# Key and value gradients of one-query attention: chunk transposes as plain matmuls into 32-bit half tiles, with other PSUM banks

## The chip, the cores and the metric

The kernel runs on one core of a Trainium2 chip. The time is that of the device for one execution, in microseconds (us). Five engines of the core work side by side, each through its own list of instructions in order: TensorE (PE, matrix products; its weight loads are listed apart as PEld), VectorE (DVE), ScalarE (ACT), GpSimd (POOL) and SyncE (SP), which here only issues transfers. Sixteen DMA engines move data between the chip's main memory (HBM) and the core's SBUF; every large transfer is cut over all sixteen. Matrix products land in PSUM, eight banks of 2 KB in each of 128 partitions.

## What is computed

Attention with a single query, and its gradients, for 64 heads (2 x 32), 8192 keys and values of 128 numbers, in bf16:

```python
B, H, Sq, Sk, D = 2, 32, 1, 8192, 128
scores = jnp.einsum("bhqd,bhkd->bhqk", q, k) * scale     # scale = D ** -0.5
p = softmax(scores, axis=-1)
out = jnp.einsum("bhqk,bhkd->bhqd", p, v)
out, vjp = jax.vjp(forward, q, k, v)
return out, *vjp(grad_out)                               # out, dq, dk, dv
```

Written out for one head, with g for grad_out: P = softmax(scale K q), grad P = V g, delta = sum(P grad P), dS = P (grad P - delta). The outputs are out = P V, dq = scale K^T dS, and two outer products as large as the inputs: dv = P g^T and dk = scale dS q^T. K and V are read once (2 MB each for a head) and dk and dv written once (2 MB each): 537 MB for all heads.

## The kernel before

A head's K and V lie in SBUF as tiles `kt` and `vt`, 128 partitions of 64 keys (NT = 64) of 128 numbers. Both pools have five buffers (UNITS). The two outer products are written in place: dv over `vt`, dk over `kt`, and these tiles are stored.

The order of the work is written out by hand (`tc.manual_schedule`, L299): no planner moves anything, each engine executes its instructions in the order of the source, and waits between engines are put in from the tiles that are read and written. The main loop (L302) runs over 65 iterations; in iteration h the scores and grad P of head h (`y`) are made and head h - 1 (`x`, index `p`) is finished. An iteration has eight steps j, one for each chunk of 16 key blocks (CH = 16): steps 0 to 3 work through K, steps 4 to 7 through V.

- `transposes` (L110): TensorE transposes 16 blocks of 128 x 128 into a bf16 PSUM tile `tp` (2 banks, two buffers); ScalarE copies the tile to SBUF as `ev` (L118).
- `products` (L122): one step later, 16 matmuls with a transposed block as weights and the one column q (or g) write 16 columns of `sdpw`. This tile is one bank for a head: scores, grad P, the transposed maxima, the broadcast maximum, the sums and the combined outputs all lie in it; it has two buffers.
- `row_max`, `all_max`, `exps` (steps 4, 5, 6): maximum over the scores, turned and broadcast by TensorE, then Exp on ScalarE with the row sums. `to_weights` casts P into `wz`, a tile that is zero but for 4 of 32 columns, so that eight heads (OG = 8) accumulate in different rows of one bank.
- `deltas`, `sums`, `weights` (steps 0, 1 of the next iteration): delta, 1/l, dS and the factors of the outer products on VectorE.
- `weighted_rows` (L229): 32 matmuls of a head, 512 columns wide, in four column groups of the array, sum P V and dS K into the banks `acc0` and `acc1`. Every eighth head `acc_to_sbuf` and `combine` (8 f32 matmuls) bring out the outputs of eight heads.
- `outer` (L263): eight VectorE products of 128 x 2048 a head, 1.2 us each, one in steps 1, 2, 4, 5, 6 and 7 and two in step 3.
- SP's queue: `store` of dv (step 3), `store` of dk (step 7), then the two loads of head h + 3 (`load`, L108), which need the buffers of head h - 2 and so wait until its stores have landed. The last head is stored in halves.
- `spread_rows` (L136), every fourth head: q and g are broadcast to all partitions through a buffer of `tp`.

PSUM holds two banks `acc`, two `sdpw` and four `tp`.

Of the kernel before, what the change touches and what calls it, by code (L numbers as in the profile page):

```python
# [10 lines left out]
AX = mybir.AxisListType  # L11
BF16 = mybir.dt.bfloat16
F32 = mybir.dt.float32

CH = 16
QG = 4
OG = 8
UNITS = 5
# [3 lines left out]
def kernel(  # L22
# [11 lines left out]
    nc = tc.nc  # L34
# [6 lines left out]
    assert NT * P == Sk and NT == 4 * CH and BH <= P and BH % QG == 0  # L41
    assert BH % OG == 0 and OG * 4 == 32
    NS = 2 * NT // CH
# [9 lines left out]

    pick = const.tile([P, 4, OG], F32)
    idv = ident_f[:].rearrange("p (g k j) -> p g j k", g=4, k=OG)
    nc.vector.tensor_copy(out=pick[:], in_=idv[:, 0])
    for g in range(1, 4):
# [7 lines left out]
    kvp = ctx.enter_context(tc.tile_pool(name="kv", bufs=UNITS))  # L65
    evp = ctx.enter_context(tc.tile_pool(name="ev", bufs=3))
    work = ctx.enter_context(tc.tile_pool(name="work", bufs=2))
    rowp = ctx.enter_context(tc.tile_pool(name="rows", bufs=2))
    ps_acc = ctx.enter_context(tc.tile_pool(name="ps_acc", bufs=1, space=bass.MemoryType.PSUM))
    ps_sdp = ctx.enter_context(tc.tile_pool(name="ps_sdp", bufs=2, space=bass.MemoryType.PSUM))  # L70
    ps_tp = ctx.enter_context(tc.tile_pool(name="ps_tp", bufs=2, space=bass.MemoryType.PSUM))
# [5 lines left out]

    MT0 = 2 * NT
    MB0 = MT0 + P
    LS0 = MB0 + 1  # L80
    CB0 = LS0 + 2
    SDPW = CB0 + 2 * OG

    acc = [ps_acc.tile([P, 4 * D], F32, name=f"acc{i}", tag=f"acc{i}") for i in range(2)]
    qT_all = const.tile([P, BH], BF16)
# [5 lines left out]
    wz = [  # L91
        [const.tile([P, NT // 4, 4 * OG], BF16, name=f"wz{w}{k}") for k in range(OG)]
        for w in range(2)
    ]
    colsT = [const.tile([P, BH], BF16, name=f"colsT{i}") for i in range(2)]
    class Head:
# [12 lines left out]

    def transposes(h, j):  # L110

        x = heads[h]
        w, c = divmod(j, NS // 2)
        tp = ps_tp.tile([P, CH, P], BF16, name="tp", tag="tp")
        for i in range(CH):
            nc.tensor.transpose(tp[:, i, :], x.kv[w][:, c * CH + i, :], ident_bf[:])  # L116
        ev = evp.tile([P, CH, P], BF16, name="ev", tag="ev")
        nc.scalar.copy(out=ev[:], in_=tp[:])  # L118
        x.ev = getattr(x, "ev", {})
        x.ev[j] = ev  # L120

    def products(h, j):  # L122
        x = heads[h]
        w, c = divmod(j, NS // 2)
        if j == 0:
            x.sdpw = ps_sdp.tile([P, SDPW], F32, name="sdpw", tag="sdpw")
            x.sdp = x.sdpw[:, 0 : 2 * NT].rearrange("p (a n) -> p a n", a=2)
        ev = x.ev.pop(j)
        col = (qT_all, doT_all)[w][:, h : h + 1]
        for i in range(CH):  # L130
            n = c * CH + i
            nc.tensor.matmul(  # L132
                x.sdp[:, w, n : n + 1], lhsT=ev[:, i, :], rhs=col, start=True, stop=True
            )
# [18 lines left out]
    def row_max(x):  # L153
        x.mp = work.tile([P, 1], F32, name="mp", tag="mp")
        nc.vector.reduce_max(out=x.mp[:], in_=x.sdp[:, 0, :], axis=AX.X)  # L155

    def all_max(x):
        mT = x.sdpw[0:1, MT0 : MT0 + P]
        nc.tensor.transpose(mT, x.mp[:], ident_f[:])
        x.gm = work.tile([1, 1], F32, name="gm", tag="gm")  # L160
        nc.vector.reduce_max(out=x.gm[:], in_=mT, axis=AX.X)  # L161

    def exps(x):
        mb = x.sdpw[:, MB0 : MB0 + 1]
        nc.tensor.matmul(mb, lhsT=ones_f[0:1, :], rhs=x.gm[:], start=True, stop=True)  # L165
        negm = work.tile([P, 1], F32, name="negm", tag="negm")
        nc.vector.tensor_scalar(out=negm[:], in0=mb, scalar1=-scale, scalar2=None, op0=ALU.mult)  # L167
        x.E = work.tile([P, NT], F32, name="E_f", tag="E_f")
        x.ld = work.tile([P, 2], F32, name="ld", tag="ld")
        nc.scalar.activation(  # L170
            out=x.E[:],
            in_=x.sdp[:, 0, :],
            func=ACT.Exp,
            bias=negm[:],
            scale=scale,
            accum_out=x.ld[:, 0:1],
        )

    def to_weights(h, w, src):
        k = h % OG  # L180
        nc.vector.tensor_copy(  # L181
            out=wz[w][k][:, :, 4 * k : 4 * k + 4],
            in_=src[:].rearrange("p (m j) -> p m j", j=4),
        )

    def deltas(x):
        junk = work.tile([P, NT], BF16, name="junk", tag="junk")
        nc.vector.tensor_tensor_reduce(  # L188
            out=junk[:],
            in0=x.E[:],  # L190
            in1=x.sdp[:, 1, :],
            scale=1.0,
            scalar=0.0,
            op0=ALU.mult,
            op1=ALU.add,
            accum_out=x.ld[:, 1:2],
        )

    def sums(x):
        x.lsum = x.sdpw[:, LS0 : LS0 + 2]  # L200
        nc.tensor.matmul(x.lsum, lhsT=ones_f[:], rhs=x.ld[:], start=True, stop=True)  # L201

    def weights(h):
# [10 lines left out]
        nc.vector.scalar_tensor_tensor(  # L214
            out=dSu[:], in0=x.sdp[:, 1, :], scalar=negdelta[:], in1=x.E[:],
            op0=ALU.add, op1=ALU.mult,
# [12 lines left out]
    def weighted_rows(h, w, chunks):  # L229


        rows, k = heads[h].kv[1 - w], h % OG
        for c in chunks:
            for g in range(4):
                n = c * CH + 4 * g
                nc.tensor.matmul(  # L236
                    acc[w][32 * g : 32 * g + 32, :],
                    lhsT=wz[w][k][:, n // 4, :],
                    rhs=rows[:, n : n + 4, :].rearrange("p n d -> p (n d)"),
                    start=(k == 0 and c == 0),  # L240
                    stop=(k == OG - 1 and c == NT // CH - 1),
                    tile_position=(0, 32 * g),
                )

    def acc_to_sbuf(x, w):
        sb = work.tile([P, 4 * D], F32, name="accsb", tag=f"accsb{w}", bufs=1)
        nc.vector.tensor_copy(out=sb[:], in_=acc[w][:])  # L247
        x.accsb = getattr(x, "accsb", {})
        x.accsb[w] = sb

    def combine(h, w):

        x = heads[h]
        c = x.sdpw[:, CB0 + w * OG : CB0 + (w + 1) * OG]
        for j in range(4):
            nc.tensor.matmul(  # L256
                c, lhsT=x.accsb[w][:, j * D : (j + 1) * D], rhs=pick[:, j, :],
                start=(j == 0), stop=(j == 3),
            )
        own = slice(h - OG + 1, h + 1)  # L260
        nc.vector.tensor_mul(out=colsT[w][:, own], in0=c, in1=rl_all[:, w, own])  # L261

# [36 lines left out]
    with tc.manual_schedule():  # L299
        for h in range(min(UNITS, BH)):  # L300
            load(h)
        for h in range(BH + 1):  # L302
# [4 lines left out]
            for j in range(NS):  # L307
                if y:
                    transposes(h, j)
                if x and j == 1:  # L310
                    sums(x)
                if y and j == 5:
                    all_max(y)
                if y and j == 6:
                    exps(y)
                if x and j < 4:
                    weighted_rows(p, j // 2, (2 * (j % 2), 2 * (j % 2) + 1))
                if x and j == 0:
                    products(p, NS - 1)
                    deltas(x)  # L320
                if y and j:
                    products(h, j - 1)
                if y and j == 4:
# [3 lines left out]
                if x:  # L327
                    if j == 1:
                        weights(p)
                        outer_and_store(p, 0, 0)  # L330
                    elif j == 2:
                        outer_and_store(p, 0, 1)
                    elif j == 3:
                        outer_and_store(p, 0, 2)
                        outer_and_store(p, 0, 3)
                    elif j > 3:
                        outer_and_store(p, 1, j - 4)
                    if full and j in (4, 5):
                        acc_to_sbuf(x, j - 4)
                    if full and j in (6, 7):  # L340
                        combine(p, j - 6)
                if j == 7:
# [4 lines left out]
        for w, dst in enumerate((o_rows, dq_rows)):  # L347
            tps = ps_tp.tile([BH, P], BF16, name="tps", tag="tp")
            nc.tensor.transpose(tps[:], colsT[w][:], ident_bf[:])
            rows = const.tile([BH, D], BF16, name=f"rows{w}")  # L350
            nc.scalar.copy(out=rows[:], in_=tps[:])
            nc.scalar.dma_start(out=dst, in_=rows[:])
# [30 lines left out]
```

## Time and profile before

| | |
|---|---|
| Time, median of 3 runs | 1311.24 us (1307.66 to 1312.27) |
| The profiled execution | 1311.96 us, span 1310.2 us |
| TensorE busy / weight loads | 1088.4 us (83%) / 893.3 us (68%) |
| ScalarE, VectorE, GpSimd busy | 984.5 us (75%), 746.9 us (57%), 8.5 us (1%) |
| Mean granted TensorE clock | 0.828 |
| Moved between HBM and SBUF | 268.5 MB read, 268.5 MB written, 410 GB/s over the span |

The profile is one execution, recorded by the hardware. Its page gives the busy time of each engine, the busy time in 40 equal slices with the granted clock and the DMA rate, the chain of work that ended last, and groups of instructions by source line: line, engine, operation, output <- input, shape, count, then busy time and mean duration in ns, then the idle time in front and what ended it. The trace behind it can be asked for stages (busy time of PE, PEld, DVE, ACT and POOL, then clock, DMA share, GB/s), for waits (who waited for whom: us in total, times, longest) and for transfers (count, KB each, median us from issue to landing). A DMA share of 1.00 says that all sixteen engines had a packet under way, not at which rate. Times are in us from the start of the span.

### The profile page before, as it was taken

The numbers are of one execution on the slowest core, as the hardware profiler recorded it, in microseconds if no ns is written. First come the engines' busy times: TensorE is split into PE (matmuls) and PEld (weight loads), VectorE is DVE, ScalarE is ACT, GpSimd is POOL, SyncE is SP. The second block draws the span as 40 slices with busy tenths as digits, with TensorE's granted clock in tenths as the row PEclk, the third lists the DMA queues.
The fourth block names the chain that finished last, engine by engine and source line by source line (L and its number), as shares of the span: only waits on it lengthen the run. The fifth ranks groups of instructions, "written<-read, shape, count | busy, mean of one in ns | idle before, by whom it ended". The sixth has DMA issues, their size and how long they took to land.

```text
span 1310.2 us, 41065 instructions
## 1 busy us (share of the span) xinstructions
PE 1088.4 (83%) x18948; PEld 893.3 (68%) x18948; DVE 746.9 (57%) x1383; ACT 984.5 (75%) x659; POOL 8.5 (1%) x24
## 2 busy tenths in 40 slices
PE   5888888888888888888888888888888888888783
PEld 4766776766776766766777676776777766666672
DVE  2655646655655655556556556465565656465564
ACT  5777868878778776778868788688777878687771
POOL 2000000000000000000000000000000000000000
PEclk9887879888888887878878789788888889798885
DMA  9999999999999999999999999999999999999995
GB/s 396 405 379 427 406 428 402 425 427 428 427 428 428 428 429 427 403 429 426 426 410 415 429 426 427 418 417 427 425 412 419 423 414 408 407 408 403 406 371 231
DMA packets 37644, 539.57 MB, mean 412 GB/s; under 512 B 4448, under 2 KB 4448, under 8 KB 4448
## 3 DMA queue, kind: packets, MB, share of 16 engines
q1 hardware_dynamic: 37152, 536.89, 97.9%
q8 instruction: 148, 2.42, 0.7%
q14 instruction: 24, 0.20, 0.0%
q10 hardware_dynamic: 320, 0.07, 0.0%
HBM read 268.47 MB, written 268.47 MB: 410 GB/s over the span
## 4 chain that ended last, share of the span: by engine, by line
PE 57%; ACT 23%; DMA 12%; DVE 4%; issue 2%; ACTq 0%; SPq 0%
PE tp L116 31%; ACT ev L118 22%; PE sdpw L132 13%; PE acc L236 10%; DMA out_dram<-kt 7%; DMA kt<-in_k_dram 4%; DVE kt L268 3%; PE sdpw L256 2%; ACT E_f L170 1%; PE sdpw L201 1%; DMA nat<-in_grad_out_dram 1%; PE pb L141 1%; DVE accsb L247 0%; DVE gm L161 0%; DVE vt L268 0%
## 5 line engine op out<-in xcount | busy, mean ns | idle before, releaser
L118 ACT COPY ev<-tp 128x2048 bf16<-128x2048 bf16 x512 | 947.8, 1866 | 290.0 <-PE tp L116 273.8
L132 PEld LDWEIGHTS <-ev 128*128 128x128 bf16 x8192 | 260.9, 99 | 328.8 <-issue 244.3
L116 PE MATMUL tp<-ident_bf,kt 128*128 128x128 bf16 x4096 | 340.9, 250 | 12.9 <-DMA kt<-in_k_dram 7.1
L116 PE MATMUL tp<-ident_bf,vt 128*128 128x128 bf16 x4096 | 311.9, 237 | 0.8 <-issue 0.8
L268 DVE TENSOR_TENSOR kt<-qd,dS 128x2048 bf16<-128x2048 bf16 x256 | 310.5, 1213 | 0.2 <-DVE mp L155 0.2
L116 PEld LDWEIGHTS <-kt 128*128 128x128 bf16 x4096 | 296.0, 114 | 19.6 <-issue 11.0
L268 DVE TENSOR_TENSOR vt<-qd,P 128x2048 bf16<-128x2048 bf16 x256 | 295.8, 1216 | 0.0
L132 PE MATMUL sdpw<-doT_all,ev 128*128 128x1 bf16 x4096 | 145.2, 165 | 172.6 <-ACT E_f L170 128.5
L116 PEld LDWEIGHTS <-vt 128*128 128x128 bf16 x4096 | 268.6, 107 | 1.0 <-issue 1.0
L188 DVE CUSTOM_DVE_ANT_0 junk<-E_f,sdpw 128x64 bf16<-128x64 f32 x64 | 14.1, 221 | 293.1 <-PE sdpw L132 293.1
L132 PE MATMUL sdpw<-qT_all,ev 128*128 128x1 bf16 x4096 | 141.6, 164 | 6.3 <-ACT ev L118 2.4
L236 PE MATMUL acc<-vt,wz 128*32 128x512 bf16 x1024 | 100.0, 476 | 0.0
L236 PE MATMUL acc<-kt,wz 128*32 128x512 bf16 x1024 | 81.3, 397 | 0.1
L236 PEld LDWEIGHTS <-wz 128*32 128x32 bf16 x2048 | 32.1, 98 | 27.8 <-issue 12.3
L206 DVE RECIPROCAL rl_all<-sdpw 128x1 f32<-128x1 f32 x64 | 10.8, 168 | 70.0 <-PE sdpw L201 70.0
L155 DVE TENSOR_REDUCE mp<-sdpw 128x1 f32<-128x64 f32 x64 | 14.4, 224 | 57.6 <-PE sdpw L132 57.6
L167 DVE TENSOR_SCALAR negm<-sdpw 128x1 f32<-128x1 f32 x64 | 10.1, 158 | 43.0 <-PE sdpw L165 42.2
L181 DVE CAST wz<-E_f 128x64 bf16<-128x64 f32 x64 | 12.4, 194 | 38.9 <-ACT E_f L170 38.9
L256 PE MATMUL sdpw<-pick,accsb 128*128 128x8 f32 x128 | 29.5, 359 | 5.8 <-DVE accsb L247 4.8
L256 PEld LDWEIGHTS sdpw<-pick,accsb 128*128 128x128 f32 x128 | 28.3, 325 | 6.8 <-DVE accsb L247 5.7
L261 DVE TENSOR_TENSOR colsT<-sdpw,rl_all 128x8 bf16<-128x8 f32 x16 | 2.7, 166 | 38.6 <-PE sdpw L256 38.6
L165 PE MATMUL sdpw<-gm,ones_f 1*128 1x1 f32 x128 | 24.2, 256 | 0.0
(39 smaller groups left out, 304.4 us busy)
## 6 DMA issues: line engine op xcount, KB each, us to landing
kt<-in_k_dram SPq DMA_DIRECT2D x64, 2048.0 KB, 24.8
vt<-in_v_dram SPq DMA_DIRECT2D x64, 2048.0 KB, 29.3
out_dram<-vt SPq DMA_DIRECT2D x63, 2048.0 KB, 25.7
out_dram<-kt SPq DMA_DIRECT2D x63, 2048.0 KB, 23.0
out_dram<-vt SPq DMA_DIRECT2D x2, 1024.0 KB, 12.7
out_dram<-kt SPq DMA_DIRECT2D x2, 1024.0 KB, 12.0
out_dram<-rows ACTq DMA_DIRECT2D x2, 16.0 KB, 5.7
nat<-in_q_dram ACTq DMA_DIRECT2D x1, 16.0 KB, 8.0
```

The lines of the kernel that those rows point to most:

```text
L116: nc.tensor.transpose(tp[:, i, :], x.kv[w][:, c * CH + i, :], ident_bf[:])
L118: nc.scalar.copy(out=ev[:], in_=tp[:])
L132: nc.tensor.matmul(x.sdp[:, w, n : n + 1], lhsT=ev[:, i, :], rhs=col, start=True, stop=True)
L141: nc.tensor.matmul(pb[:, i].rearrange("p a d -> p (a d)"), lhsT=ident_bf[0:BH, h : h + 1].to_broadcast([BH, P]), rhs=nat[:].rearrange("p a ...
L155: nc.vector.reduce_max(out=x.mp[:], in_=x.sdp[:, 0, :], axis=AX.X)
L165: nc.tensor.matmul(mb, lhsT=ones_f[0:1, :], rhs=x.gm[:], start=True, stop=True)
L170: nc.scalar.activation(out=x.E[:], in_=x.sdp[:, 0, :], func=ACT.Exp, bias=negm[:], scale=scale, accum_out=x.ld[:, 0:1],)
L188: nc.vector.tensor_tensor_reduce(out=junk[:], in0=x.E[:], in1=x.sdp[:, 1, :], scale=1.0, scalar=0.0, op0=ALU.mult, op1=ALU.add, accum_out= ...
L201: nc.tensor.matmul(x.lsum, lhsT=ones_f[:], rhs=x.ld[:], start=True, stop=True)
L236: nc.tensor.matmul(acc[w][32 * g : 32 * g + 32, :], lhsT=wz[w][k][:, n // 4, :], rhs=rows[:, n : n + 4, :].rearrange("p n d -> p (n d)"), ...
L256: nc.tensor.matmul(c, lhsT=x.accsb[w][:, j * D : (j + 1) * D], rhs=pick[:, j, :], start=(j == 0), stop=(j == 3),)
L268: nc.vector.tensor_tensor(out=x.kv[1 - w][:, n : n + CH, :].rearrange("p n (d t) -> p n d t", t=2), in0=row.unsqueeze(1).to_broadcast([P, ...
```

## The change

- Each transpose is a plain matmul with the identity as the moving operand; `tp` is f32 and holds eight blocks (a half chunk, HC = 8) in the same 2 banks. `ev` is a half chunk in bf16, with five buffers for three.
- Of a head's 16 copies of half chunks ScalarE makes 14 and VectorE two: the second halves of steps 0 and 7.
- An iteration's step is split in halves u = 0, 1: transposes, products and weighted rows alternate by half chunk.
- Four heads (OG = 4) share one bank `acc` for both sums: P takes the first 16 of 32 columns of `wz`, dS the last 16. Both outputs of four heads are combined in one bank `c`.
- The scores lie in a bank `sm`, grad P and the sums in a bank `dp`, one buffer each.
- The outer products move: step 1 has one, steps 2 and 3 two, steps 4, 5 and 6 one, step 7 none. Stores are issued behind the same products as before, so in steps 3 and 6.

```diff
-    def transposes(h, j):
+    def transposes(h, j, u):
...
-        tp = ps_tp.tile([P, CH, P], BF16, name="tp", tag="tp")
-        for i in range(CH):
-            nc.tensor.transpose(tp[:, i, :], x.kv[w][:, c * CH + i, :], ident_bf[:])
-        ev = evp.tile([P, CH, P], BF16, name="ev", tag="ev")
-        nc.scalar.copy(out=ev[:], in_=tp[:])
+        tp = ps_tp.tile([P, HC, P], F32, name="tp", tag="tp")
+        for i in range(HC):
+            n = c * CH + u * HC + i
+            nc.tensor.matmul(
+                tp[:, i, :], lhsT=x.kv[w][:, n, :], rhs=ident_bf[:], start=True, stop=True
+            )
+        ev = evp.tile([P, HC, P], BF16, name="ev", tag="ev")
+        if u and j in (0, 7):
+            nc.vector.tensor_copy(out=ev[:], in_=tp[:])
+        else:
+            nc.scalar.copy(out=ev[:], in_=tp[:])
...
-        if j == 0:
-            x.sdpw = ps_sdp.tile([P, SDPW], F32, name="sdpw", tag="sdpw")
-            x.sdp = x.sdpw[:, 0 : 2 * NT].rearrange("p (a n) -> p a n", a=2)
+        if c == 0 and u == 0:
+            if w:
+                x.dp = ps_one.tile([P, NT + 2], F32, name="dp", tag="dp")
+            else:
+                x.sm = ps_one.tile([P, NT + P + 1], F32, name="sm", tag="sm")
...
-            out=wz[w][k][:, :, 4 * k : 4 * k + 4],
+            out=wz[w][k][:, :, 16 * w + 4 * k : 16 * w + 4 * k + 4],
...
-                    acc[w][32 * g : 32 * g + 32, :],
+                    acc[32 * g : 32 * g + 32, :],
...
-                    start=(k == 0 and c == 0),
-                    stop=(k == OG - 1 and c == NT // CH - 1),
+                    start=(w == 0 and k == 0 and c == 0),
+                    stop=(w == 1 and k == OG - 1 and c == NT // CH - 1),
...
             for j in range(NS):
-                if y:
-                    transposes(h, j)
...
+                for u in range(2):
+                    if y:
+                        transposes(h, j, u)
+                    if u == 0:
+                        if x and j == 1:
+                            sums(x)
+                        if y and j == 5:
+                            all_max(y)
+                        if y and j == 6:
+                            exps(y)
+                    if y and j:
+                        products(h, j - 1, u)
+                    elif x and j == 0:
+                        products(p, NS - 1, u)
+                    if x and j < 4:
+                        weighted_rows(p, j // 2, (2 * (j % 2) + u,))
+                if x and j == 0:
+                    deltas(x)
...
                 if x:
-                    if j == 1:
-                        weights(p)
-                        outer_and_store(p, 0, 0)
-                    elif j == 2:
-                        outer_and_store(p, 0, 1)
-                    elif j == 3:
-                        outer_and_store(p, 0, 2)
-                        outer_and_store(p, 0, 3)
-                    elif j > 3:
-                        outer_and_store(p, 1, j - 4)
-                    if full and j in (4, 5):
-                        acc_to_sbuf(x, j - 4)
-                    if full and j in (6, 7):
-                        combine(p, j - 6)
+                    for i in ((), (0,), (1, 2), (3, 4), (5,), (6,), (7,), ())[j]:
+                        outer_and_store(p, i // 4, i % 4)
+                    if full and j == 4:
+                        acc_to_sbuf(x)
+                    if full and j == 6:
+                        combine(p)
```

The remaining lines carry the new names (`x.sm` and `x.dp` for `x.sdp`, one `colsT`, `pick` and `c` with both outputs) through.

## The prediction

> **What bounds the kernel now.** I read the page's totals first, then the busy times by stage, the waits, the transfers by stage, and two single heads. All durations come from the one profiled execution: span 1310.2 us, 1311.96 us as timed, so 1.8 us lie around the span; it stands 0.7 us above the median of 1311.24. A measurement of this kernel can tell about 0.5% (6.6 us) from no change.
>
> The stages, whose last three columns are the granted TensorE clock, the share of the DMA engines and GB/s:
>
> ```profile
> 0.00:60.00 60.00, 41.80 (x679) 34.66 (x680) 24.30 (x43) 37.51 (x25) 8.55 (x24) 0.86 0.98 407
> 60.00:100.00 40.00, 34.56 (x648) 28.20 (x646) 25.07 (x45) 32.82 (x23) 0.00 (x0) 0.87 0.93 375
> 240.00:520.00 280.00, 239.64 (x4179) 197.17 (x4177) 162.45 (x304) 216.49 (x145) 0.00 (x0) 0.83 1.01 428
> 960.00:1240.00 280.00, 235.00 (x4137) 192.77 (x4135) 161.86 (x302) 215.32 (x144) 0.00 (x0) 0.84 1.00 412
> 1240.00:1310.00 70.00, 44.33 (x672) 33.99 (x669) 34.75 (x63) 32.64 (x23) 0.00 (x0) 0.67 0.75 308
> ```
>
> The reader sees that the DMA engines have no idle time from 100 to 1240 us. A head moves 8.39 MB (two loads and two stores of 2.10 MB), so 428 GB/s is 19.6 us for a head. The totals of the waits and, below them, SP's waits in 960 to 1240:
>
> ```profile
> PE sdpw L132 <- ACT E_f L170: 128.5, 64, 2.1
> PE sdpw L132 <- DVE gm L161: 43.4, 64, 1.5
> PE tp L116 <- DMA kt<-in_k_dram: 7.1, 4, 2.4
> ```
>
> ```profile
> SPq L108 <- DMA out_dram<-kt: 196.1, 14, 18.9
> SPq L276 <- DVE kt L268: 53.4, 16, 9.2
> ```
>
> TensorE almost never waits for a load (7.1 us), so compute looks like the bound; yet late in the run the loads themselves stand in SP's queue for 14 us a head, until an old store has landed and freed their buffer. The landing times say why. Issues of 100 to 240, 240 to 520 and 960 to 1240 us, one line of each (last number: us to landing):
>
> ```profile
> out_dram<-kt SPq DMA_DIRECT2D x7, 2048.0 KB, 11.0
> ```
>
> ```profile
> out_dram<-kt SPq DMA_DIRECT2D x14, 2048.0 KB, 20.0
> ```
>
> ```profile
> out_dram<-kt SPq DMA_DIRECT2D x14, 2048.0 KB, 36.1
> ```
>
> The trace holds the 16 completion marks of each transfer, one from each DMA engine. The last mark comes 2.7 us after the first at 65 us, 2.9 at 236, 14.7 at 530, and 17 to 19 from 944 to the end: one engine falls behind steadily. From 236 to 540 us its marks are 5.067 us apart (20.27 us a head) and the foremost engine's 4.86 (19.45). From 78 us its marks follow each other with no step over 6.6 us up to 1309.2, 1 us before the end. So the slowest DMA engine sets the time. Compute matters only where it leaves that engine dry (two steps of 6.2 and 7.8 us behind 64.5), and a second way: when the backlog reaches 18 us, loads wait for it, the other fifteen engines run dry together each head, start together, and 16 KB packets that take 0.611 us then take 0.8 to 1.5 us in bursts. From 944 to 1284 us the slowest engine itself needs 5.159 us a transfer (66 of them in 340.5 us), 20.64 a head.
>
> Two heads show compute, one undisturbed, one in a stretch where the clock fell to 0.5:
>
> ```profile
> 598.80:616.90 18.10, 15.44 (x293) 13.05 (x293) 11.28 (x22) 15.05 (x11) 0.00 (x0) 0.91 1.01 430
> 656.00:682.00 26.00, 23.31 (x327) 19.18 (x324) 12.48 (x25) 15.83 (x12) 0.00 (x0) 0.67 1.01 430
> ```
>
> Store issues at 239.8 and 932.7 us lie 35 heads apart: 19.8 us a head for compute, mixed from such heads.
>
> **The change part by part.** Rows used:
>
> ```profile
> L118 ACT COPY ev<-tp 128x2048 bf16<-128x2048 bf16 x512 | 947.8, 1866 | 290.0 <-PE tp L116 273.8 <-ACT ev L118 1.4
> L149 ACT CAST qd<-pb 128x1024 bf16<-128x1024 f32 x16 | 16.2, 1016 | 8.1 <-PE pb L141 8.1
> L247 DVE COPY accsb<-acc 128x512 f32<-128x512 f32 x16 | 10.8, 678 | 0.0
> L155 DVE TENSOR_REDUCE mp<-sdpw 128x1 f32<-128x64 f32 x64 | 14.4, 224 | 57.6 <-PE sdpw L132 57.6
> ```
>
> *ScalarE.* Eight copies a head of 1.866 us (14.9) become 14 of half size. The L149 row is exactly such a copy, 1.016 us: 14.2 us. With Exp and its sum (0.52) and a quarter of the L149 copy (0.25) ScalarE needs 15.0 us a head, 0.7 less.
>
> *VectorE.* Two copies of 128x1024 are added. From the PSUM rows, (678 - 224)/(512 - 64) is 1.01 ns an element, so 1.2 us each (bounds: 1.016 as ScalarE, 1.36 as twice 678): 2.4 us a head on 11.7 (746.9/64), 14.1 in all. They are hidden while VectorE stays under ScalarE's 15.0. Queued behind each are delta and the weights (at j = 0) and the cast of P (at j = 7); who waits is TensorE at `sums`, and at the next half tile, since the copy holds one of two PSUM buffers. I take 1.2 us a head for that.
>
> *TensorE.* The 128 transposes become as many matmuls with the same operands and columns. Sixteen transposes take 0.92 us at full clock (57.5 ns each). From above: the L141 matmul writes 32-bit output from 256 columns, four in 1.03 us at half clock, so 65 ns for 128 columns at full clock, +1.0 us a head. From below: 16 products with one column take 0.48 us, 30 ns each, -3.5 us. The row with the same columns is nearest, so I take no change. In the trace the clock falls to 0.5 in 64 stretches that sum to 452 us although TensorE is busy 83% of the span. [...]
>
> *Own banks.* The products of grad P no longer write the bank that Exp and the maximum read: 2.0 and 0.7 us a head of waits go. What is late next is ScalarE's chain of half copies, 15.0 us. So a head of compute lies between 15.0 and the present 18.1 us undisturbed; with VectorE's 1.2 us and the wait at `sums` I take 17. With the clock as uneven as now (+1.7, from 19.8 against 18.1) it would be 18.7. Both are under 19.45, so the transfers hide either one.
>
> *Sums of four heads.* The combine in f32 runs 16 times with both outputs in one, against 8 times two; matmuls (128 rows), copies (16) and products with 1/l are as many or fewer. Nothing, hidden in the same way. GpSimd clears 8 tiles for 16 before the first load lands at 12 us: nothing.
>
> *Moved outer products.* One is done earlier from j = 2 on, so a head's stores are issued at j = 3 and 6 for 3 and 7. SP's order (store, store, load, load) and its 258 issues stay; no transfer is moved past another, none gets smaller.
>
> *What this does to the slowest engine.* Faster compute never leaves it dry in 65 to 236 us: its 33 transfers there take 33 x 5.067 = 167.2 for 171.6 us, -4.4. But now the others run at 4.86 from the start, the backlog grows by 0.2 us a transfer from 2.7 us, and reaches 18.5 after 78 transfers, at 460 us and not at 944. From there each of 166 remaining transfers (244 less 78; four half ones counted as two) costs 5.159. Sum: 64.5 + 78 x 5.067 + 166 x 5.159 = 1316.1, +1.0 to the end of the span, +1.8 around it: 1318.9; less 0.7 as the medians go, **1318 us**. With the bounds of the late stage, 20.53 (944 to 1149) and 20.81 a head (from 1149), it is 1314 to 1326; I take 1308 to 1328 as this case's own range.
>
> **The rivals.**
>
> 1. *The backlog grows, but without the bursts*: the slow packets came from VectorE's late stores in that stage (53.4 us of SP's waits), which faster compute ends. Against it: from 1196 us on all four issues of a head came within 2.4 us and the bursts stayed. Then 64.5 + 244 x 5.067 + 2.8 = 1303.6, less 0.7: 1303 (1299 to 1309).
> 2. *No engine falls behind*, for the backlog came with compute's uneven pace. 536.9 MB at 428 GB/s is 1254, 2.4 lost in the first 20 us (376 GB/s), 19 at the end (1260 to 1310 moved what 31 us hold): 1276, timed 1277. Against it: the engine fell behind evenly for 300 us with no gap in the others. [...]
> 3. *Slower: the half tile that VectorE copies stalls the ring.* VectorE runs in order; a copy can stand behind an outer product (1.2 us), and takes 1.2; with one of two buffers held, TensorE and then ScalarE stop. Twice a head this is up to 4.8 us: 17 + 4.8 = 21.8, and 64 heads, 12 us to the first load and 16 at the end make 1423. It decides from 20.3 us a head, that is from 3.3 us of stall, and from 1.6 us if the clock stays as uneven as now. For it: VectorE's 14.1 us leave little room; against it: it idles 43% today.
> [...]
>
> **How the numbers follow.** The forecast 0.50, rival 1 0.20, rival 2 0.08, rival 3 0.22 (rival 4 lies inside the forecast). The forecast's range puts about 0.45 of it within 0.5% (up to 1317.8) and the rest above; rival 1 is 0.6 faster (below 1304.7), 0.4 same. So faster 0.20, same 0.31, slower 0.49. The range from 1299 leaves out rival 2 and little of rival 1; up to 1355 it leaves out the worse half of rival 3.
>
> **What would show it.** Right: ScalarE's copies near 1.02 us and VectorE's near 1.2; the wait on Exp gone; TensorE waiting for loads for some us a head; SP's loads waiting for stores from 460 us on, with 36 us to a store's landing and 405 to 415 GB/s. Wrong: landing times that stay near 20 us with 425 GB/s to the end (rivals 1, 2), or SP waiting for VectorE's outer products in most heads and a DMA share under 0.97 (rival 3).

## The result and the profile after

The changed kernel takes 1326.8 us (median, 1325.41 to 1328.14) against 1309.45 us (1306.97 to 1312.27) for the kernel before in the same session: ratio 1.0132, 95% interval 1.0105 to 1.0159, so 1.3% slower. The forecast was 1318 us, 0.5% above the time before; the rise is more than twice as large. The profiled execution took 1328.14 us, span 1326.3 us.

The stages after (us; busy time of PE, PEld, DVE, ACT, POOL; granted clock, DMA share, GB/s):

```profile
60.00:100.00 40.00, 36.34 (x676) 30.60 (x674) 31.05 (x53) 32.50 (x40) 0.00 (x0) 0.98 1.01 427
240.00:520.00 280.00, 235.70 (x4081) 192.59 (x4082) 189.19 (x325) 194.38 (x222) 0.00 (x0) 0.91 1.01 423
960.00:1240.00 280.00, 236.12 (x3909) 193.88 (x3907) 181.36 (x310) 186.87 (x217) 0.00 (x0) 0.85 1.00 401
```

Early the change gains: 427 GB/s for 375 in 60 to 100 us. From 240 us on it loses: 423 for 428, then 401 for 412, with the DMA engines as busy as ever. Compute did become faster. The half-chunk copies, and one undisturbed head (Exp to Exp takes 17.3 us in such heads):

```profile
L119 ACT CAST ev<-tp 128x1024 bf16<-128x1024 f32 x896 | 879.2, 1026 | 379.3 <-PE tp L112 364.4
L117 DVE CAST ev<-tp 128x1024 bf16<-128x1024 f32 x128 | 156.7, 1224 | 298.5 <-PE tp L112 293.5
```

```profile
150.00:168.00 18.00, 16.11 (x309) 13.30 (x306) 14.32 (x25) 14.58 (x18) 0.00 (x0) 1.00 1.01 428
```

The chain of work that ended last, by engine (before: PE 57%, ACT 23%, DMA 12%), then the waits in total of the matmuls of L112, then SP's waits in 960 to 1240 us:

```profile
DMA 63%; PE 21%; ACT 8%; DVE 4%; issue 1%; SPq 1%; ACTq 0%; DVEq 0%
```

```profile
PE tp L112 <- DMA kt<-in_k_dram: 115.1, 49, 4.4
...
PE tp L112 <- ACT ev L119: 38.0, 112, 0.6
```

```profile
SPq L103 <- DMA out_dram<-kt: 262.7, 14, 19.5
SPq L278 <- DVE kt L270: 3.8, 6, 1.2
```

TensorE now waits for loads (115.1 us for 7.1), and the loads stand behind a store that has not landed in every head of that stage (262.7 us in 14 heads), while waits for VectorE's products have nearly gone (3.8 us for 53.4). Landing times of the store of `kt`, issued in 100 to 240, 240 to 520 and 960 to 1240 us:

```profile
out_dram<-kt SPq DMA_DIRECT2D x7, 2048.0 KB, 25.7
```

```profile
out_dram<-kt SPq DMA_DIRECT2D x14, 2048.0 KB, 39.5
```

```profile
out_dram<-kt SPq DMA_DIRECT2D x14, 2048.0 KB, 40.2
```

They were 11.0, 20.0 and 36.1 us. The transfer 78 places behind the one that lands at 64 us has its last completion mark 2.7 us earlier than in the kernel before (462.2 for 464.9 us), the very last one 16.2 us later (1325.4 for 1309.2): all that is lost is lost behind 460 us.

The marks show how (the figures are counted from the trace's records of single marks and packets). Call *lag* the time from the first to the last mark of one transfer. It reaches 17 us at 395 us (before: 697 us) and stays at 18 to 19. Up to there the slowest engine needs 20.5 us a head and the foremost 19.45; behind it both need the same: 20.5, from about 700 us on 21.0. In the same steps 16 KB packets get longer. What they take beyond 0.611 us, summed over all packets in 100 us, is 11 us from 60 to 360 us; 28, 49, 61 and 71 in the next four hundreds; then 94 to 103 from 760 to 1260. In the kernel before it is 64 and 34 in the two hundreds from 60 us, 10 to 27 from 260 to 960 us, then 38, 69, 91. Meanwhile the other engines draw together: the mean lag of the middle one, the eighth of the sixteen to finish, falls from 6.6 us (360 to 460 us) to 0.8 (from 760 on).

### The profile page after: what moved, and what is told of

It reads as the page before. It is cut to its first block, busy times and chain, and to the rows that moved or that the text cites. A ratio compares the mean times of both kernels' runs of the same rounds, so it can differ in the third digit from the quotient of the medians.

```text
span 1326.3 us, 42070 instructions
## 1 busy us (share of the span) xinstructions
PE 1108.8 (84%) x18948; PEld 909.2 (69%) x18948; DVE 887.3 (67%) x1511; ACT 906.7 (68%) x1043; POOL 4.8 (0%) x16
## 3 DMA queue, kind: packets, MB, share of 16 engines
q8 instruction: 148, 2.42, 0.6%
## 4 chain that ended last, share of the span: by engine, by line
DMA 63%; PE 21%; ACT 8%; DVE 4%; issue 1%; SPq 1%; ACTq 0%; DVEq 0%
DMA out_dram<-kt 36%; DMA kt<-in_k_dram 27%; PE tp L112 13%; ACT ev L119 8%; PE acc L240 5%; DVE ev L117 3%; PE sm L135 2%; DMA nat<-in_grad_out_dram 1%; PE dp L205 1%; DVE kt L270 1%; PE dp L135 1%; SPq L103 0%; SPq L278 0%; PE sm L169 0%; DVE vt L270 0%
## 5 line engine op out<-in xcount | busy, mean ns | idle before, releaser
L119 ACT CAST ev<-tp 128x1024 bf16<-128x1024 f32 x896 | 879.2, 1026 | 379.3 <-PE tp L112 364.4
L112 PE MATMUL tp<-ident_bf,kt 128*128 128x128 bf16 x4096 | 379.9, 247 | 119.2 <-DMA kt<-in_k_dram 115.1
L112 PEld LDWEIGHTS <-kt 128*128 128x128 bf16 x4096 | 280.2, 110 | 256.0 <-issue 133.8
L117 DVE CAST ev<-tp 128x1024 bf16<-128x1024 f32 x128 | 156.7, 1224 | 298.5 <-PE tp L112 293.5
L112 PE MATMUL tp<-ident_bf,vt 128*128 128x128 bf16 x4096 | 313.4, 219 | 48.2 <-ACT ev L119 38.0
L135 PEld LDWEIGHTS <-ev 128*128 128x128 bf16 x8192 | 333.0, 100 | 2.2 <-issue 0.2
L112 PEld LDWEIGHTS <-vt 128*128 128x128 bf16 x4096 | 259.1, 98 | 81.6 <-issue 73.1
L135 PE MATMUL dp<-doT_all,ev 128*128 128x1 bf16 x4096 | 180.3, 165 | 0.1
L135 PE MATMUL sm<-qT_all,ev 128*128 128x1 bf16 x4096 | 178.0, 164 | 0.0
L240 PE MATMUL acc<-vt,wz 128*32 128x512 bf16 x1024 | 127.8, 489 | 4.7 <-DVE wz L185 4.5
L240 PE MATMUL acc<-kt,wz 128*32 128x512 bf16 x1024 | 106.1, 407 | 0.5 <-DVE wz L185 0.5
L205 PE MATMUL dp<-ld,ones_f 128*128 128x2 f32 x128 | 27.8, 287 | 10.4 <-DVE ld L192 9.5
L153 ACT CAST qd<-pb 128x1024 bf16<-128x1024 f32 x16 | 16.2, 1012 | 12.3 <-PE pb L145 12.3
L169 PE MATMUL sm<-gm,ones_f 1*128 1x1 f32 x128 | 24.2, 256 | 0.0
## 6 DMA issues: line engine op xcount, KB each, us to landing
out_dram<-kt SPq DMA_DIRECT2D x63, 2048.0 KB, 39.5
```

The lines of the kernel that those rows point to most:

```text
L112: nc.tensor.matmul(tp[:, i, :], lhsT=x.kv[w][:, n, :], rhs=ident_bf[:], start=True, stop=True)
L117: nc.vector.tensor_copy(out=ev[:], in_=tp[:])
L135: nc.tensor.matmul((x.dp if w else x.sm)[:, n : n + 1], lhsT=ev[:, i, :], rhs=col, start=True, stop=True,)
L153: nc.scalar.copy(out=qd[:], in_=pb[:])
L240: nc.tensor.matmul(acc[32 * g : 32 * g + 32, :], lhsT=wz[w][k][:, n // 4, :], rhs=rows[:, n : n + 4, :].rearrange("p n d -> p (n d)"), sta ...
```

## The experiments

Theory A, the prediction's: one DMA engine is slower than the rest and falls behind as long as transfers run freely; faster compute only lets it reach its limit sooner. Rival B: something that the change itself does (f32 reads of PSUM, half-chunk copies, other banks) slows the transfers. Later C, D and D' came up, as told in place.

**1. Slower compute** (the changed kernel):

```diff
+    idle = const.tile([P, 8, P], BF16)
...
+                if y and j in (1, 3, 5):
+                    m = 4 if j == 5 else 8
+                    nc.scalar.copy(out=idle[:, :m, :], in_=ones_f[:].unsqueeze(1).to_broadcast([P, m, P]))
```

> The kernel after, with three added ScalarE copies of a constant (2.6 us a head) whose result nobody reads, so that compute goes at about 19.8 us a head, as before the change, and not at 17.3. Theory A (the backlog of the slowest DMA engine: faster compute lets the transfers run ahead to their limit early, from there fifteen engines run dry together each head and packets lengthen in bursts): the limit comes late or not at all, and the kernel gets FASTER, 1304 to 1316 us. Rival B (the change's own traffic, 32-bit PSUM tiles, VectorE's copies, the higher clock, slows the transfers whatever compute's pace): 1325 to 1340 us.

Measured: 1314.78 us (1312.08 to 1318.11), 1.0047 of before (1.0025 to 1.0069): with 2.6 us a head more on ScalarE it is 12 us faster than without. Its stage 960 to 1240 us:

```profile
960.00:1240.00 280.00, 236.93 (x4190) 195.93 (x4190) 197.25 (x334) 229.98 (x274) 0.00 (x0) 0.94 1.00 413
```

ScalarE has 43 us more in the late stage, and the rate there is 413 GB/s for 401. Lag reaches 17 us at 688 us, as before the change. All of the change's traffic is still there, so B can't be the cause of the 12 us; A holds as to the pace. The 0.5% that are left above the kernel before this run doesn't explain.

**2. One part alone** (the kernel before, with a bank of their own for scores and for grad P, one buffer each; bf16 transposes and whole-chunk copies as before):

```diff
-            x.sdpw = ps_sdp.tile([P, SDPW], F32, name="sdpw", tag="sdpw")
+            x.sm = ps_sdp.tile([P, NT + P + 1 + 2 * OG], F32, name="sm", tag="sm")
+        if j == NS // 2:
+            x.dp = ps_sdp.tile([P, NT + 2 + 2 * OG], F32, name="dp", tag="dp")
```

> The kernel before, with one part of the change alone: scores and grad P in banks of their own with one buffer each, so that TensorE's 2.0 and 0.7 us of waits a head go. Transposes, whole chunks, ScalarE's copies and the banks of the sums stay. Theory A: compute gets faster by 1 to 2 us a head, the backlog reaches its limit at 400 to 700 us and not at 944, and the kernel gets SLOWER than before, 1314 to 1326 us. Rival B: none of the suspected traffic is there, 1305 to 1312 us.

Measured: 1334.71 us (1331.13 to 1337.94), 1.0195 (1.0164 to 1.0227). Its stage 960 to 1240 us:

```profile
960.00:1240.00 280.00, 228.28 (x3913) 179.93 (x3912) 152.79 (x286) 200.29 (x136) 0.00 (x0) 0.80 1.00 400
```

The direction is A's, the size is beyond what I gave it. Own banks alone bring a head of compute from 18.1 to 15.1 us (Exp to Exp, undisturbed), less than the whole change has (17.3). Lag reaches 17 us at 361 us and the late pace is 21.1 us a head: the faster the compute, the slower the kernel. The other parts of the change, f32 half chunks above all, are not needed for the loss.

**3. Relief for the slow engine** (the changed kernel; every fifth store of dv cut into 120 and 8 partitions, to take packets from one engine):

```diff
-        nc.sync.dma_start(out=(dv_v, dk_v)[w][h][:, a:b, :], in_=heads[h].kv[1 - w][:, a:b, :])
+        dst, src = (dv_v, dk_v)[w][h], heads[h].kv[1 - w]
+        for lo, hi in ((0, 120), (120, P)) if w == 0 and h % 5 == 2 else ((0, P),):
+            nc.sync.dma_start(out=dst[lo:hi, a:b, :], in_=src[lo:hi, a:b, :])
```

> The kernel after, with the store of dv of every fifth head issued as two transfers, 120 partitions and 8. The first should use fifteen of the sixteen DMA engines and the second eight, so that one engine moves eight packets (4.9 us) less in five heads. Theory A, if the engine left out is the slow one: its lag of 0.9 us a head is taken back, landing times stay under 30 us, GB/s near 425 to the end, 1275 to 1300 us. Theory A, if another engine is the slow one: the lag is as before and the time 1324 to 1335 us. Rival B: 1324 to 1335 us.

Measured: 1401.67 us (1389.38 to 1409.27), 1.0698 (1.0628 to 1.0769), outside both expectations. The rate in 40 slices of 80 to 130 us, around the first such store:

```profile
GB/s 419 419 419 367 380 288 288 315 367 406 393 406 367 459 433 419 380 367 288 341 393 433 433 433 419 406 446 406 433 419 433 446 446 419 419 433 426 406 419 419
```

It falls to 288 GB/s where the part of 120 partitions is moved, and the lag jumps from 3.8 to 9 us. The transfer meant as relief is itself slow, so the run tells nothing on A. That 120 partitions go over fifteen engines was an estimate from the 128 packets of 16 KB of a whole transfer, eight for each of its sixteen completion marks; which engines moved them this run does not show.

**4. The transfers alone** (loads and stores in SP's order; scores, gradients and outer products are left out):

```diff
...
+            if x:
+                for w in range(2):
+                    store(p, w)
+            if x and UNITS <= h + 3 < BH:
+                load(h + 3)
```

> Only the transfers of the kernel after, in SP's order with the same buffers: loads of K and V, stores of the same tiles one iteration later; scores, gradients and outer products are left out, so dk and dv are copies of v and k. Theory A: the lag and the bursts need no compute, the store of a kt tile lands after 34 to 40 us from about 400 us on, 395 to 415 GB/s, 1300 to 1330 us. Rival B: without compute's traffic the transfers go at 428 GB/s, 1262 to 1285 us.

Measured: 1254.84 us (1253.93 to 1255.18), 0.9585 (0.9562 to 0.9608). Late stage, and the landing of its stores of `kt`:

```profile
960.00:1240.00 280.00, 0.00 (x0) 0.00 (x0) 0.00 (x0) 0.00 (x0) 1.00 1.01 431
```

```profile
out_dram<-kt SPq DMA_DIRECT2D x15, 2048.0 KB, 37.5
```

The queue is as deep as it can be, with stores landing after 37.5 us; yet the slowest engine needs 19.5 us a head and the lag is 4.0 us at most. So A fails where it took an engine to be slow by itself. Running ahead is needed for the loss, but what holds an engine back comes with compute.

**5 and 6. The transfers with code.** The queue `q8`, of kind instruction, carries 148 packets of 16 KB in the changed kernel and in the one before. That is 2.42 MB for TensorE's 37,896 matmuls and weight loads, 64 bytes each; the bare transfers have none. Theory C: this code, fetched by the DMA engines that move the data, is what holds one back. Rival D: the data traffic of the engines in SBUF and PSUM does. Added to run 4, with 296 and then 592 for N:

```diff
+            if y:
+                t = ps_one.tile([P, 8], F32, name="t", tag="t")
+                for i in range(N):
+                    nc.tensor.matmul(
+                        t[0:1, i % 8 : i % 8 + 1], lhsT=ident_bf[0:1, 0:1],
+                        rhs=y.kv[0][0:1, i % NT, 0:1], start=True, stop=True,
+                    )
```

> The bare transfers of the run before (1254.84 us; slowest engine 19.45 us a head, last completion mark at most 3.8 us after the first), with 296 matmuls of one row and one column a head added, so that TensorE's instruction stream is as long as in the changed kernel (37,894 rows of PE) while next to no data moves on chip. Scores, gradients and outer products are left out, as before. Theory C (instruction code is fetched through the DMA engines, 148 packets of 16 KB in the changed kernel, and each delays the data packet beside it on one engine by about 0.45 us; 148 x 0.45 / 64 = 1.04 us a head): the slowest engine needs 20.3 to 20.6 us a head, the lag climbs to about 18 us, and the time is 1300 to 1330. Rival D (the lag comes from the engines' own data traffic in SBUF and PSUM): lag under 5 us and 1250 to 1262.

Measured with 296: 1288.80 us (1288.46 to 1289.15), 34 us above the bare transfers.

```profile
q8 instruction: 148, 2.42, 0.7%
```

Lag grows to 17 us at 570 us, the slowest engine needs 20.06 us a head: C in kind, and D falls, as next to no data moves on chip here. The size is half of what C gave (0.23 us a packet for 0.45); the packets hardly lengthen here (8 us in 100 us before the limit, 23 to 32 behind it).

> The same with 592 such matmuls a head (75,782 rows of PE); by the products' row, 30 ns each, TensorE needs 17.8 us a head for them, so it should still not set the pace. Theory C: twice the code packets (about 296), the slowest engine at 21.3 to 21.6 us a head, and 1365 to 1400. Rival D: as the bare transfers, 1250 to 1262. Should TensorE need more than 20 us a head for them, the completion marks and not the time decide.

Measured with 592: 1682.27 us (1676.47 to 1685.25), missed by both. Code packets and TensorE's waits:

```profile
q8 instruction: 296, 4.85, 1.1%
```

```profile
PE t L312 <- issue: 671.6, 250, 5.6
```

"issue" is time in which an engine waits for nothing that the profile shows: TensorE stands so 250 times, for 2.7 us each. That it waits for code then is the author's guess, which no view shows. It sets the time (26.4 us a head), so the run says nothing on the lag.

**7. The changed kernel with less code.** The transposes and scores computed are those of one block repeated; the tiles written and copied and all transfers stay as they were.

```diff
-        for i in range(HC):
+        for i in range(0, HC, 4):
...
-                tp[:, i, :], lhsT=x.kv[w][:, n, :], rhs=ident_bf[:], start=True, stop=True
+                tp[:, i : i + 4, :], lhsT=x.kv[w][:, n, :],
+                rhs=ident_bf[:].unsqueeze(1).to_broadcast([P, 4, P]), start=True, stop=True,
...
+            (x.dp if w else x.sm)[:, n : n + HC], lhsT=ev[:, 0, :],
+            rhs=col.to_broadcast([P, HC]), start=True, stop=True,
```

> The changed kernel with the eight transposing matmuls of a half chunk written as two of 512 columns and its eight products as one of eight columns: the same tiles are written, read and copied, with 10,586 rows of PE instead of 37,674. The transposes and the scores are then those of one block repeated, so the numbers computed are others; the work of the other engines and all transfers are the same. Theory C: code packets fall to about a third, the slowest engine needs about 19.8 us a head, the lag stays under 10 us for most of the run, and the time is 1265 to 1290. Rival D: the data traffic is the same, so 1320 to 1330 with a lag of 18 us from 400 us on.

Measured: 1275.46 us (1274.87 to 1275.75), 0.9741 (0.9723 to 0.9758): C's range. Code packets, and the late stage:

```profile
q8 instruction: 44, 0.72, 0.2%
```

```profile
960.00:1240.00 280.00, 210.59 (x1226) 81.15 (x1226) 192.62 (x330) 192.08 (x229) 0.00 (x0) 0.86 1.00 423
```

VectorE and ScalarE do at least as much in that stage as in the changed kernel (192.6 and 192.1 us for 181.4 and 186.9), and the data still move faster (423 GB/s for 401). But this run also reads fewer weights, which is rival D'.

**8. The code back as filler.** To run 7, 212 matmuls of one row and column a head (`cf[0:1, ...]`, `lhsT=ident_bf[0:1, 0:1]`) were added between the half chunks.

> The run with less code (1275.46 us, 44 code packets), with 212 matmuls of one row and one column a head added, spread over the half chunks, so that TensorE has 37,722 instruction rows, as in the changed kernel, while its weight loads and all data traffic stay as in the run with less code. Transposes and scores are again those of one block repeated. Theory C (the code packets delay the data): about 148 code packets, the slowest engine at 20.3 to 20.6 us a head before the limit and up to 21 after it, and 1315 to 1332. Rival D' (the run with less code was faster because TensorE read fewer weights from SBUF): 1270 to 1282.

Measured: 1546.85 us (1450.51 to 1584.96), inconclusive. In 1000 to 1300 us:

```profile
1000.00:1300.00 300.00, 299.62 (x3382) 139.94 (x3380) 154.38 (x261) 165.53 (x185) 0.00 (x0) 0.56 0.79 322
```

TensorE has no pause in this execution (1584.96 us) and its clock is down to 0.56: compute sets the time, and the transfers never ran freely.

**9. Less code in the products alone** (the last part of run 7's edit).

> The changed kernel with only the eight products of a half chunk written as one of eight columns (the scores are those of one block repeated): 22,874 instruction rows, about 90 code packets. Theory C, on the line between 44 packets (1275.5) and 148 (1326.8), 0.49 us a packet: 1293 to 1304. Rival D' (weights read): it loads 112 of 256 weight tiles fewer a head where the run with less code loaded 208 fewer, so by that line 1299 as well; this run alone tells a line from a threshold: 1320 or more, or 1280 or less, would be one.

Measured: 1298.43 us (1296.82 to 1299.73), 0.9902 (0.9868 to 0.9936), with 92 packets of code. So 44, 92 and 148 packets give 1275.5, 1298.4 and 1326.8 us: a line, 0.48 and 0.51 us a packet. D' expected it too.

**10 to 12. The same code with other weights.** Run 9, with seven matmuls of their own results beside each product: of one row and column in run 10, of 128 rows and W = 32 or 128 columns in runs 11 and 12. All three have the changed kernel's 148 code packets. As it stands in runs 11 and 12:

```diff
...
+        for i in range(HC - 1):
+            nc.tensor.matmul(
+                cf[0:W, 16 + i : 17 + i], lhsT=ev[:, 1 + i, 0:W], rhs=col,
+                start=True, stop=True,
+            )
```

> The run before (one product of eight columns for eight of one; 1298.43 us, 92 code packets) with seven matmuls of one row and one column added beside each such product, which read next to no data: 37,210 instruction rows, as the changed kernel has, with 112 of its 256 wide weight loads a head gone and less TensorE work than it has. The scores are again those of one block repeated. Theory C (the code packets set the lag): 148 code packets again, the slowest engine at 20.3 to 20.6 us a head up to the limit and 20.5 to 21 after it, 1318 to 1332. Rival D' (the fewer weight reads were what helped): 1293 to 1304, as the run before. Should compute set the pace (TensorE's clock falls with such small matmuls), TensorE waits for no loads and the completion marks decide.

Measured: 1314.84 us (1307.87 to 1320.63), between the two. Its late stage and SP's waits in it:

```profile
960.00:1240.00 280.00, 270.45 (x3971) 211.07 (x3970) 183.87 (x314) 190.70 (x220) 0.00 (x0) 0.78 0.99 412
```

```profile
SPq L283 <- DVE kt L275: 102.6, 14, 11.2
SPq L283 <- DVE vt L275: 92.3, 12, 10.8
```

TensorE is busy 97% of the stage at a clock of 0.78, and stores wait 195 us for VectorE's products: compute sets the pace again, as in run 1. The case that the expectation named had come, and the lag's growth (17 us at 486 us) shows only that there is more of it than with 92 packets (571 us).

> The run before (seven small matmuls beside each product of eight columns) with the small ones made wider: each reads its own transposed block, all 128 rows and 32 of its 128 columns, as weights, and the one column q or g. 37,210 instruction rows and 148 code packets as in the changed kernel, a quarter of the weight bytes of its products; the scores are again those of one block repeated. Theory C (the code packets alone): the slowest engine at 20.4 to 20.6 us a head up to the limit, 1320 to 1332. Rival D' (the weight reads): 20.1 to 20.3 us and 1296 to 1308. If TensorE is slowed again by small matmuls (hardly any waits for loads), the pace of the completion marks before the limit decides.

> The same with all 128 columns of the block as weights: instruction rows, code packets and weight bytes are those of the changed kernel; only the products' results go elsewhere. Both theories: as the changed kernel, 1322 to 1331, slowest engine 20.5 us a head before the limit. Another time would say that the place of the results, one bank for all, matters.

Measured: 1329.27 us (1323.12 to 1330.19) with 32 columns, ratio 1.0128 (1.0093 to 1.0164), and 1327.17 us (1323.34 to 1330.23) with 128, ratio 1.0124 (1.0093 to 1.0155). TensorE waits for loads as in the changed kernel, here with 32 columns:

```profile
PE tp L113 <- DMA kt<-in_k_dram: 96.3, 46, 4.1
```

The slowest engine needs 20.49 and 20.44 us a head before the limit. A quarter of the products' weight bytes with the same code costs as much as all of them: D' falls, and with run 9, which differs from run 11 by these short matmuls, 14,336 instructions more (56 code packets) are worth some 30 us.

The series together (pace of the slowest engine from about 230 us until the lag reaches 17 us):

| Run | Code packets | Slowest engine, us a head | Lag reaches 17 us at | Time, us |
|---|---|---|---|---|
| 4, transfers alone | 0 | 19.5 | never | 1254.8 |
| 7, less code | 44 | 19.85 | 906 us | 1275.5 |
| 9, less code in the products | 92 | 20.13 | 571 us | 1298.4 |
| 5, transfers and code | 148 | 20.06 | 570 us | 1288.8 |
| before | 148 | 20.27 | 697 us | 1309.5 |
| 1, slower compute | 148 | 20.36 | 688 us | 1314.8 |
| 10, weights 1 wide (compute sets the pace) | 148 | 20.32 | 486 us | 1314.8 |
| after | 148 | 20.54 | 395 us | 1326.8 |
| 12, weights 128 wide | 148 | 20.44 | 395 us | 1327.2 |
| 11, weights 32 wide | 148 | 20.49 | 445 us | 1329.3 |
| 2, own banks alone | 148 | 20.63 | 361 us | 1334.7 |

Of the kernels that compute, those with the same code differ by the pace of their compute, and those that wait for transfers with compute like the changed kernel's by their code, that is by the number of TensorE's instructions.

**What the packets tell.** All these runs count packets of code and TensorE's instructions together. The traces tell them apart, in the stretch before the limit.

- *The code packets do not go over the slowest engine.* One costs the engine that carries it 1.3 to 1.4 us: its own 0.93, and 0.4 to 0.5 by which the data packet behind it is longer. In the changed kernel 22 of them come from 200 to 395 us, and no step of the slowest engine's lag there is over 0.63 us. Other engines carry them. In run 5, at 560 us, seven engines are within 0.6 us of the foremost, eight lie 10.9 to 13.1 us behind it, and the slowest 16.6.
- *The slowest engine loses its time in stores.* In the changed kernel its lag grows by 0.49 us over each store of dv and 0.53 over each store of dk, and by 0.01 and 0.02 over the loads: its 16 KB packets of stores are longer than 0.611 us, and so they are with no code packet under way. The mean step of a store is 0.19 us in run 7 (44 packets' worth of instructions), 0.35 in run 9 (92) and 0.51 in the changed kernel (148). Two such steps in each of 64 heads would be 24, 44 and 65 us; these three lie 21, 44 and 72 us above the bare transfers.
- *They are longer while TensorE's instructions run.* Run 5 has a head's matmuls in one stretch of some 10 us. In these three stretches the slowest engine works on a load, then on the store of dv, then on that of dk:

```profile
320.00:324.00 4.00, 4.00 (x166) 4.00 (x163) 0.00 (x0) 0.00 (x0) 1.00 1.01 434
326.00:330.00 4.00, 3.01 (x115) 2.90 (x114) 0.00 (x0) 0.00 (x0) 1.00 0.99 422
331.00:335.00 4.00, 0.00 (x0) 0.00 (x0) 0.00 (x0) 0.00 (x0) 1.00 1.01 430
```

Its packets take 0.611, then 0.64 to 0.76, then 0.611 us. So it is from 200 to 570 us, over the 55 of 73 transfers that can be followed packet by packet: 0.72 us on the mean for packets of dv stores with 34 or more of TensorE's instructions beside them, 0.612 for those of dk stores with none, 0.611 for loads with 34 or more. Theory C had the right count and the wrong carrier: before the limit it is TensorE's running instructions, and not the transport of their code, that go with the slowest engine's delay. By what path they do is not shown. Nor can any run exclude that it is the recording of the instructions for the profile: every run here has a recorded span and clock.

## Why the prediction was right in kind and too low

- *Compute.* Right: ScalarE's copies 1.026 us (1.016 forecast), VectorE's 1.224 (1.2), 17.3 us a head (17); the wait on Exp no longer stands among the waits. Rival 3 did not come: SP's wait for VectorE's products fell to 3.8 us in 960 to 1240.
- *The clock.* It rose, from 0.83 to 0.91 in 240 to 520 us and to 1.00 in undisturbed heads (150 to 168 us); the stretches at 0.5 went from 452 to 295 us. Run 2, which keeps the bf16 transposes, has 0.83 in 240 to 520 us. So the rise came with parts of the change that run 2 leaves out; which of them brought it no run shows. That every head would have the undisturbed clock, as the 17 us a head took it, was the author's assumption. It is 0.85 in 960 to 1240 us, where TensorE waits for loads. The loss does not need the higher clock: run 2 has it at 0.80 in the same stage.
- *The early gain*, -4.4 us from 65 to 236 us: confirmed, as the transfer that is done at 236 us before is done at 231 now.
- *Transfers up to the limit*: forecast 78 at 5.067 us from 64.5 to 459.7 us. Measured, they take from 64.2 to 462.2 us, 5.103 each: the forecast's end of this part is 2.5 us too early. The lag was at 17 us by 395 and at 18 by 416 us, where the forecast had the limit at 460, since the slowest engine needs 20.54 us a head and not 20.27: a store of dk costs it 0.53 us and not 0.30 as before the change, with 24 of TensorE's instructions beside each packet for 16.
- *Transfers behind it*: **this is the term that was mis-sized.** Forecast 166 at 5.159 us (20.64 a head), measured 863.2 us, 5.20 each (20.8 a head): the forecast is 6.8 us too low. The two errors make up the 9.2 us between the sum's 1318.9 and the profiled 1328.1. With it went the signs named for this stage: 39.5 to 40.2 us to a store's landing (36 forecast) and 401 GB/s (405 to 415).
- *Why that size was wrong.* 5.159 was the mean over 944 to 1284 us of the kernel before, a stage in which the bursts were still growing (38, 69, 91 us of lengthening in 100 us). The changed kernel is in the grown state from 760 us on (94 to 103) and pays 21.0 us a head there. The prediction had the two halves of that stage (20.53 and 20.81) and put their mean into the sum; the later one would have given 1326. That would have been luck in part, as the changed kernel too goes through a growing state first (20.5 a head from 395 to 700 us). Why the grown state is as slow as it is stays open.
- *The bursts* were not due to VectorE's late stores (rival 1): those waits went and the bursts came sooner. Rival 2 had the right premise and the wrong condition: there is a state in which no engine falls behind, at 431 GB/s, but only run 4, with no instructions of TensorE's for the heads at all, reaches it; no change of pace did.
- *That one engine is slow by itself*, tacit in the prediction, is refuted by run 4 (lag 4.0 us at most). The change adds no instructions (37,896, in 148 packets of code, before and after): what it changed is how early the other engines may run away from the one that is held back, and, by 0.27 us a head, how much of TensorE's work falls beside that engine's stores.

## What to carry to other kernels

Where transfers set the end, as here, faster compute was not free: it filled the queue (40.2 us to a store's landing for 36.1 in 960 to 1240 us), the sixteen engines came apart by 18 to 19 us, and behind that point all of them needed 20.5 us a head, the slowest engine's pace, and 21.0 from about 700 us on. Look for the time between the first and the last completion mark of a transfer, and read the price of a new regime from where it has settled, at its end, not from its mean. And count instructions: in this kernel, which moves data all the time, each 128 short matmuls with their weight loads less (256 instructions, 16 KB of code) were worth half a microsecond (runs 7, 9 and the changed kernel), though TensorE was not the bound.

## What the runs showed of the hardware

- Code for TensorE is moved beside the data. It stands among the packets of the DMA queues as `q8`, kind instruction: 148 packets of 16 KB, 0.93 us each, in the changed kernel, 44, 92 and 296 in runs 7, 9 and 6, one for 256 of TensorE's instructions in the changed kernel. Behind each of the 22 from 200 to 395 us a data packet starts within 0.02 us of its end and takes 0.96 to 1.16 us for 0.611. So a code packet delays the engine that carries it by 1.3 to 1.4 us. In run 5 some 64 have come by 560 us (32 of them in 240 to 520 us); spread evenly over eight engines they would make 10.4 to 11.2 us each, an estimate, and eight engines lie 10.9 to 13.1 us behind the foremost there.
- One other engine loses its time in stores, where TensorE's instructions run beside them: 0.72 us a packet in stores of dv with 34 or more instructions beside it, 0.612 in stores of dk with none, 0.611 in loads with as many (run 5). 256 instructions cost 0.23 us of the run's time beside bare transfers (run 5, where the step over the store of dv, 0.52 us, gives 33 of the 34 us in 64 heads) and 0.5 us beside full compute (runs 7, 9 and the changed kernel). Which engine it is the trace does not tell. Without TensorE's instructions two engines lag, but by 3.8 us at 1100 us (run 4), the others by 0.4 at most.
- With 592 short matmuls a head beside a full load of transfers, TensorE stood idle 250 times, for 2.7 us each on the mean, with nothing shown to wait for (run 6).
- Loads and stores together ran at 431 GB/s from 60 to 1240 us with no compute beside them (run 4).
- A store of 120 partitions in place of 128 was slow: 288 GB/s around it (run 3).
- Left open: why packets of all engines lengthen when these have drawn together. It goes with code and compute: 94 to 103 us in 100 us in the changed kernel, up to 66 with 92 code packets, 11 to 17 with 44, 23 to 32 with code and no compute, at most 2 with neither. It does not need the limit: in run 1 it is 61 to 77 from 60 to 360 us, where the lag is 2 to 3 us and the middle engine's under 1, and 10 to 11 in the next three hundreds, where the engines have come apart.
